# The root of three groups' norms as a power on GpSimd in a three-layer kernel

## The chip, the cores and the metric

The kernel runs on one core of a Trainium2 chip. The time is that of one execution on the device, in microseconds, and the number to predict is the median over several executions.

## The reference

Three layers follow one another. The first is attention over clusters: each query and each key is assigned to the centroid that its direction is nearest to, and a query sees only keys of its own cluster. The other two are networks over the 1536 tokens; the last mixes 8 experts with gates that are normalised in turns over rows and columns.

```python
B, H, S, D, C = 2, 8, 768, 64, 16
q_n = q / (np.linalg.norm(q, axis=-1, keepdims=True) + 1e-06)
k_n = k / (np.linalg.norm(k, axis=-1, keepdims=True) + 1e-06)
c_n = centroids / (np.linalg.norm(centroids, axis=-1, keepdims=True) + 1e-06)
q_assign = np.argmax(np.einsum('bhsd,hcd->bhsc', q_n, c_n), axis=-1)
k_assign = np.argmax(np.einsum('bhsd,hcd->bhsc', k_n, c_n), axis=-1)
mask = q_assign[:, :, :, None] == k_assign[:, :, None, :]
scores = np.where(mask, scale * np.matmul(q, k.transpose(0, 1, 3, 2)), -1e9)
attn = np.exp(scores - max); attn = attn / (sum(attn) + 1e-09); out = attn @ v
...
h = x @ w_in; r = np.maximum(h, 0.0); x = (s * (r * r) + b) @ w_out
...
for e in range(E): out += P[:, e:e+1] * (np.maximum(x @ w1[e], 0.0) @ w2[e])
```

## The kernel before

The work has two stages. The attention stage takes the first 280 us or so, the two networks the rest; the networks are almost only matrix products.

In the attention stage the 16 heads of the two batches make four groups of four heads (`n` = 0 to 3 in the code; the first to fourth group here). Every head has six query tiles of 128 rows, so there are 96 tiles, `g` = 0 to 95, and a group lasts 24 of them. `tile_steps(g)` issues for each tile: `row_max` two tiles ahead (VectorE, L454), `expo` one tile ahead (ScalarE, L461), `transp` (TensorE, L476), `score` three tiles ahead (TensorE, L448), the copy of the transposed weights out of PSUM in a rounded high part on ScalarE (`ath`, L483) and a remainder on VectorE (`atl`, L489), and a third of the product with the values (TensorE, L501). A score tile `s` has two buffers in PSUM, so the next score but one waits until `expo` has read its tile.

Before a group's heads can be scored their queries and keys have to be assigned. `prepare(n)` does it: it rounds the inputs into `hi` and `lo`, multiplies with the centroids (`sims`, L282), turns the result (`turn`, L290), scales it with the inverse norms (`normal`, L297), takes the maximum over the clusters (`top`, L301), marks where it is reached (`match`, `back`, `earliest`) and stacks `hi`, `lo` and the marks into `qa`, `qb`, `ka`, `kb` by transfers from SBUF to SBUF (`stack`, L331; those of the third and fourth head of the first group are issued from GpSimd's queue, all others from SP's).

`norms(n)` gives the inverse norms of a group in a tile `rn` of 128x48: it loads the group's queries and keys a second time with rows on partitions, squares them, sums over the 64 columns (`total`, L229 to L234, on GpSimd, VectorE or both, by group), takes the root (`root`, L237, on ScalarE), adds 1e-6 and inverts (`inverse`, L240 and L243, on VectorE). The first two groups' norms are made before the first tile; the second group's `inverse` is issued just ahead of tile 0's work, and its addition is held in program order:

```python
def root():
    nc.scalar.activation(rn, rn, AF.Sqrt)

def inverse():
    add = nc.vector.tensor_scalar_add(rn, rn, 1e-6)
    if n == 1:
        self.tc.keep_in_program_order(add)
    nc.vector.reciprocal(rn, rn)
```

For the third and fourth group these steps are put between the tiles by a table of offsets: `root` at tile 25 for the third group and at tile 50 for the fourth, `inverse` after it. ScalarE evaluates a function from a table that has to be loaded first (ACT_TABLE_LOAD): the root's and the exponent's are different tables; in this trace copies and squares cause no load. Each engine runs its instructions in a fixed order. Up to tile 71 a scheduler makes that order from the program and its dependencies; from there on the program's order is kept.

Of the kernel before, what the change touches and what calls it, by code (L numbers as in the profile page):

```python
# [8 lines left out]
F32 = mybir.dt.float32  # L9
# [3 lines left out]
AF = mybir.ActivationFunctionType  # L13
ALU = mybir.AluOpType
# [3 lines left out]
P = 128  # L18
# [44 lines left out]
class Kernel:  # L63
# [88 lines left out]
    def more_constants(self):  # L152
        nc, per = self.nc, self.per
        self.ones = per.tile([P, P], F32, name="ones")
        nc.gpsimd.memset(self.ones, 1.0)
        self.sb = per.tile([P, 2], F32, name="sb")
        self.wg = per.tile([P, KT, NE], F32, name="wg")
        self.wgs = per.tile([P, KT, 2, NE], F32R, name="wgs")
# [43 lines left out]
    def norms(self, n, soon=False):  # L202

        nc = self.nc
        rn = self.rn[n] = self.tile("rn", [P, 24, 2], bufs=2, pool=self.prep)
        nats = {}

        def load(u):
            if n == 1:
                nats[u] = self.tile("atl" if u else "ath", [P, 12, 2, D], bufs=2)  # L210
            else:
                nats[u] = self.tile("nat", [P, 12, 2, D], bufs=2, pool=self.prep)
            b, t = divmod(n, 2)
            nc.sync.dma_start(nats[u], self.qkn[b, t, :, 12 * u : 12 * u + 12])

        def square(u):
            nat = nats[u]
            if soon:
                nc.scalar.activation(nat, nat, AF.Square)
            else:  # L220
                nc.gpsimd.tensor_tensor(nat, nat, nat, op=ALU.mult)

        def total(u):
            nat = nats.pop(u)
            width = D
            while width > (1, 1, D, D // 2)[n] and n:
                width //= 2
                add = nat[:, :, :, :width]
                nc.gpsimd.tensor_tensor(add, add, nat[:, :, :, width : 2 * width], op=ALU.add)  # L229
            out = rn[:, 12 * u : 12 * u + 12]  # L230
            if width == 1:
                nc.gpsimd.tensor_copy(out.unsqueeze(3), nat[:, :, :, :1])
            else:
                nc.vector.reduce_sum(out, nat[:, :, :, :width], axis=AX.X)  # L234

        def root():
            nc.scalar.activation(rn, rn, AF.Sqrt)  # L237

        def inverse():
            add = nc.vector.tensor_scalar_add(rn, rn, 1e-6)  # L240
# [4 lines that stand above are left out]
        return load, square, total, root, inverse  # L245

    def prepare(self, n, soon=False):
# [886 lines left out]
```

## Time and profile before

| | |
|---|---|
| median of 3 runs | 1570.52 us (1570.37 to 1571.54) |
| the profiled execution | 1570.48 us |
| its span, first to last instruction | 1568.7 us |
| TensorE busy | 1526.6 us (97%) |
| VectorE busy | 898.7 us (57%) |
| ScalarE busy | 760.3 us (48%) |
| GpSimd busy | 964.6 us (61%) |
| ACT_TABLE_LOAD on ScalarE | 6, of 1283 ns each |
| mean granted clock of TensorE | 0.995 of full speed |

In the rows further down, PE is TensorE, DVE VectorE, ACT ScalarE and POOL GpSimd. A line of the timeline has the start in us, the duration in us, the engine, the line of the code, the operation, output and inputs by the program's names, the shapes, and how many instructions it merges; in brackets stands how long the engine sat idle before it and what ended that.

### The profile page before, as it was taken

Reading aid. Unit: us, or ns where it says so; the run is one execution under the profiler, and the core shown is the slowest. Engines: PE = TensorE matmul, PEld = TensorE weight load, DVE = VectorE, ACT = ScalarE, POOL = GpSimd, SP = SyncE. Lnnn points to the kernel's source line nnn. Section 1 sums busy time; section 2 is a strip of 40 time slices with the busy share of each in tenths; the row PEclk is TensorE's granted clock in tenths of the full one; section 3 lists DMA queues with packets and bytes.
Section 4 is the critical chain, followed back from the end, with each engine's and each line's share of the span. In section 5 each row is a group of like instructions: output and inputs, shape, how many; then the busy total and the mean of one; then the engine's idle time right before and its main releaser. Section 6 shows DMA issues by size and latency. Waiting matters only on the chain.

```text
span 1568.7 us, 21863 instructions
## 1 busy us (share of the span) xinstructions
PE 1526.6 (97%) x8136; PEld 1399.6 (89%) x8136; DVE 898.7 (57%) x1573; ACT 760.3 (48%) x1416; POOL 964.6 (61%) x726
## 2 busy tenths in 40 slices
PE   4999998999999999999999999999999999999998
PEld 4888987999999988899999999999999999999997
DVE  7989889876653445644444535565445444444444
ACT  4889898866665643343333333333333333333331
POOL 5764446656664866656566666677565757575652
PEclk8999999999999999999999999999999999999999
DMA  9864440122220011112121211213121212121211
GB/s 276 196 188 102 97 125 29 54 81 81 81 108 0 1 55 68 67 54 81 56 80 58 77 66 69 78 57 121 55 81 55 81 55 81 54 81 55 81 55 41
DMA packets 26793, 124.69 MB, mean 79 GB/s; under 512 B 4448, under 2 KB 4576, under 8 KB 16448
## 3 DMA queue, kind: packets, MB, share of 16 engines
q1 hardware_dynamic: 26112, 120.95, 23.9%
q0 software_dynamic: 576, 2.36, 0.7%
q8 instruction: 64, 1.05, 0.3%
q14 instruction: 41, 0.34, 0.1%
HBM read 99.80 MB, written 3.15 MB: 66 GB/s over the span
## 4 chain that ended last, share of the span: by engine, by line
PE 87%; ACT 4%; DVE 3%; POOL 2%; issue 2%; DMA 1%; SPq 0%; ACTq 0%; POOLq 0%; DVEq 0%
PE t L135 34%; PE s L985 22%; PE y L985 11%; PE s L705 7%; PE s L448 3%; PE pv L501 3%; PE u L135 2%; PE t L476 2%; ACT e L461 1%; PE u L476 1%; DVE atl L489 1%; DVE m L454 1%; ACT ath L483 1%; POOL fa L623 0%; DMA ka<-hi 0%
## 5 line engine op out<-in xcount | busy, mean ns | idle before, releaser
L964 ACT ACTIVATE hh<-c 128x384 fp32r<-128x384 f32 x256 | 134.6, 526 | 606.1 <-PE y L985 266.4
L892 POOL TENSOR_TENSOR wl<-raw,wh 128x1024 fp32r<-128x1024 f32 x64 | 155.3, 2427 | 348.2 <-ACT wh L891 348.2
L965 DVE SCALAR_TENSOR_TENSOR hl<-c,hh 128x384 fp32r<-128x384 f32 x256 | 174.8, 684 | 172.5 <-ACT hh L964 172.5
L985 PE MATMUL s<-wh,hh 128*128 128x512 f32 x512 | 201.2, 393 | 0.0
L985 PE MATMUL s<-wl,hh 128*128 128x512 f32 x512 | 200.6, 392 | 0.0
L985 PE MATMUL s<-wh,hl 128*128 128x512 f32 x512 | 200.3, 391 | 0.0
L135 PE MATMUL t<-th,ah 128*128 128x384 f32 x512 | 171.8, 336 | 0.8 <-DVE c L1059 0.8
L135 PE MATMUL t<-tl,ah 128*128 128x384 f32 x512 | 172.0, 336 | 0.0
L135 PE MATMUL t<-th,al 128*128 128x384 f32 x512 | 171.8, 336 | 0.0
L884 POOL TENSOR_TENSOR al<-sm,ah 128x1024 fp32r<-128x1024 f32 x64 | 156.6, 2447 | 3.5 <-ACT ah L881 3.4
L882 POOL TENSOR_TENSOR al<-raw,ah 128x768 fp32r<-128x768 f32 x64 | 137.8, 2153 | 0.0
L135 PE MATMUL t<-xh,ah 128*128 128x384 f32 x384 | 129.4, 337 | 0.1
L135 PE MATMUL t<-xh,al 128*128 128x384 f32 x384 | 129.2, 336 | 0.0
L135 PE MATMUL t<-xl,ah 128*128 128x384 f32 x384 | 129.0, 336 | 0.0
L1035 DVE TENSOR_TENSOR c<-t,c 128x384 f32<-128x384 f32 x64 | 35.7, 558 | 144.9 <-PE t L135 144.9
L985 PEld LDWEIGHTS s<-wh,hl 128*128 128x128 f32 x512 | 96.1, 188 | 21.1
L985 PEld LDWEIGHTS s<-wh,hh 128*128 128x128 f32 x512 | 96.2, 188 | 11.7
L985 PEld LDWEIGHTS s<-wl,hh 128*128 128x128 f32 x512 | 96.2, 188 | 11.3
L691 POOL TENSOR_TENSOR hl<-r,hh 128x384 fp32r<-128x384 f32 x64 | 74.3, 1162 | 49.3 <-ACT r L690 46.1
L985 PE MATMUL y<-wh,hl 128*128 128x512 f32 x256 | 99.7, 390 | 0.0
L985 PE MATMUL y<-wh,hh 128*128 128x512 f32 x256 | 99.7, 389 | 0.0
L985 PE MATMUL y<-wl,hh 128*128 128x512 f32 x256 | 99.6, 389 | 0.0
(231 smaller groups left out, 4019.2 us busy)
## 6 DMA issues: line engine op xcount, KB each, us to landing
raw<-in_w SPq DMA_DIRECT2D x64, 1024.0 KB, 4.8
wraw<-in_w SPq DMA_DIRECT2D x16, 1024.0 KB, 4.9
raw<-in_qk SPq DMA_DIRECT2D x15, 384.0 KB, 5.1
ka<-hi SPq DMA_DIRECT2D x28, 192.0 KB, 3.7
nat<-in_qkn SPq DMA_DIRECT2D x6, 768.0 KB, 7.7
vraw<-in_v SPq DMA_DIRECT2D x8, 384.0 KB, 4.8
out<-x SPq DMA_DIRECT2D x12, 256.0 KB, 2.0
qa<-hi SPq DMA_DIRECT2D x14, 192.0 KB, 2.6
```

Of the source, the lines that this page charges most:

```text
L135: self.nc.tensor.matmul(out, a, b, start=(i == 0), stop=(i == n - 1))
L448: nc.tensor.matmul(s[:, u, :HALF], a[:, qs], k[:, u * HALF : u * HALF + HALF], start=(a is qa), stop=(a is qb))
L476: nc.tensor.transpose(t[:, k, :], e[:, kt * P : kt * P + P], self.ident)
L501: nc.tensor.matmul(o, vt[:, kt].rearrange("p a d -> p (a d)"), aT[half][w][:, kt, :], start=(kt == 0 and w == 0), stop=(kt == QT - 1 and w ...
L691: nc.gpsimd.tensor_tensor(hl, r, f32(hh), op=ALU.subtract)
L705: nc.tensor.matmul(o, a, b, start=(start and i == 0), stop=(stop and i == 2))
L882: nc.gpsimd.tensor_tensor(al[:, : 3 * Q], raw[:, : 3 * Q], f32(ah[:, : 3 * Q]), op=ALU.subtract)
L884: nc.gpsimd.tensor_tensor(al[:, 3 * Q :], self.sums.rearrange("p a b -> p (a b)"), f32(ah[:, 3 * Q :]), op=ALU.subtract)
L892: nc.gpsimd.tensor_tensor(wl, raw[:, 1024:], f32(wh), op=ALU.subtract)
L964: nc.scalar.activation(hh, c, AF.Relu)
L965: nc.vector.scalar_tensor_tensor(hl, c, 0.0, f32(hh), op0=ALU.max, op1=ALU.subtract)
L985: nc.tensor.matmul(ys[t][m], a, b, start=(start and i == 0), stop=(stop and i == 2))
```

## The change

The root of the second to fourth group is a power of 0.5 on GpSimd, element by element, with a column of 0.5 spread over the tile. The first group's root and that of the centroids' norms stay on ScalarE.

```diff
@@ more_constants
         self.ones = per.tile([P, P], F32, name="ones")
         nc.gpsimd.memset(self.ones, 1.0)
+        self.half = per.tile([P, 1], F32, name="half")
+        nc.gpsimd.memset(self.half, 0.5)
@@ norms
         def root():
-            nc.scalar.activation(rn, rn, AF.Sqrt)
+            if n:
+                nc.gpsimd.tensor_tensor(rn, rn, self.half.unsqueeze(2).to_broadcast([P, 24, 2]), op=ALU.pow)
+            else:
+                nc.scalar.activation(rn, rn, AF.Sqrt)
```

The line numbers below the second hunk rise by five: L237 becomes L240 and L242, L240 becomes L245, L448 L453, L454 L459, L461 L466, L483 L488.

The order of GpSimd at the second group's root, just before tile 0, with what each instruction waits for (`atl` is the buffer of squares, `qa` and `ka` are stacked heads); before:

```order
L229 TENSOR_TENSOR atl<-atl 128x24 [waits Pool_49]
L232 COPY rn<-atl 128x24 [waits Pool_49]
L331 DMA qa<-hi_116 64x768
L331 DMA qa<-lo_118 64x768 [waits DVE_49]
L331 DMA ka<-hi_120 64x768 x2
```

and now:

```order
L231 TENSOR_TENSOR atl<-atl 128x24 [waits Pool_49]
L234 COPY rn<-atl 128x24 [waits Pool_49]
L240 TENSOR_TENSOR rn<-rn,half 128x48 [waits Pool_49]
L336 DMA qa<-hi_118 64x768
L336 DMA qa<-lo_120 64x768 [waits DVE_49]
L336 DMA ka<-hi_122 64x768 x2
```

The power stands between the last sum and the transfers. On VectorE the instructions of the same place, `inverse` of the second group and the first row maxima behind it, keep their order:

```order
L344 CAST kb<-eq 16x768
L245 TENSOR_SCALAR rn<-rn 128x48 [waits Pool_49]
L248 RECIPROCAL rn<-rn 128x48 [waits DVE_49]
L459 TENSOR_REDUCE m<-s 128x1 [waits PE_49] x3
L494 TENSOR_TENSOR atl<-u,ath 128x3x128 [waits Activation_49]
```

Only the addition's wait is another: it was for ScalarE and is for GpSimd.

The order of ScalarE at the third group's root, about tile 25; before:

```order
L237 ACT_TABLE_LOAD
L237 ACTIVATE rn<-rn 128x48
L483 CAST ath<-t 128x3x128 x2
L461 ACT_TABLE_LOAD
L461 ACTIVATE e,sums_65<-s,m 128x768
L483 CAST ath<-u 128x3x128
L461 ACTIVATE e,sums_65<-s,m 128x768
L526 COPY xb<-pv 64x384
L534 COPY rs<-t 64x384
L483 CAST ath<-t 128x3x128
L483 CAST ath<-u 128x3x128
L268 CAST hi_1265<-raw 128x768
```

with the third exponential right behind these rows, and now:

```order
L488 CAST ath<-t 128x3x128 x2
L531 COPY xb<-pv 64x384
L466 ACTIVATE e,sums_65<-s,m 128x768
L488 CAST ath<-u 128x3x128
L466 ACTIVATE e,sums_65<-s,m 128x768
L539 COPY rs<-t 64x384
L488 CAST ath<-t 128x3x128
L488 CAST ath<-u 128x3x128
L466 ACTIVATE e,sums_65<-s,m 128x768
L488 CAST ath<-t 128x3x128
L273 CAST hi_1267<-raw 128x768
```

Both loads and the root are gone, the copy into `xb` stands ahead of the first exponential, and the rounding into `hi` behind the third. The fourth group's root has lost its two loads in the same way.

The order of VectorE at the third group's `top` (`mx`), about tile 33; before:

```order
L454 TENSOR_REDUCE m<-s 128x1
L509 RECIPROCAL rsum<-rsum 128x3
L240 TENSOR_SCALAR rn<-rn 128x48
L243 RECIPROCAL rn<-rn 128x48
L528 TENSOR_TENSOR xb<-pv,xb 64x384
L290 STREAM_TRANSPOSE sim<-t 128x384
L489 TENSOR_TENSOR atl<-u,ath 128x3x128
L489 TENSOR_TENSOR atl<-t,ath 128x3x128
L454 TENSOR_REDUCE m<-s 128x1
L301 TENSOR_REDUCE mx<-sim 128x48
```

and now, behind the same row maximum:

```order
L533 TENSOR_TENSOR xb<-pv,xb 64x384
L514 RECIPROCAL rsum<-rsum 128x3
L236 TENSOR_REDUCE rn<-nat 128x24
L295 STREAM_TRANSPOSE sim<-t 128x384
L494 TENSOR_TENSOR atl<-u,ath 128x3x128
L494 TENSOR_TENSOR atl<-t,ath 128x3x128
L459 TENSOR_REDUCE m<-s 128x1
L494 TENSOR_TENSOR atl<-t,ath 128x3x128
L494 TENSOR_TENSOR atl<-u,ath 128x3x128
L459 TENSOR_REDUCE m<-s 128x1
L513 TENSOR_REDUCE rsum<-sums_64 128x3
L306 TENSOR_REDUCE mx<-sim 128x48
```

The maximum over the clusters comes one row maximum later, the fourth group's `inverse` has moved behind it, out of these rows, and a sum of that group's squares has come in from earlier. The order of the transfers on SP's queue is the same in both.

## Rows read from the trace of the kernel before

**Rows 1.** Busy time by stretches: length, PE, PEld, DVE, ACT, POOL, clock, DMA, GB/s.

```profile
345.00:1565.00 1220.00, 1216.39 (x6259) 1115.28 (x6257) 598.84 (x1039) 482.24 (x829) 766.53 (x551) 1.00 0.18 65
```

**Rows 2.** Timeline, all engines, 27 to 31.7 us: the second group's root and tile 0.

```profile
27.15 0.22 POOL L232 COPY rn<-atl 128x24 f32<-128x24 f32 x1
...
27.40 0.24 ACT L237 ACTIVATE rn<-rn 128x48 f32<-128x48 f32 x1 [6.08 <-POOL rn L232]
...
28.54 0.19 DVE L240 TENSOR_SCALAR rn<-rn 128x48 f32<-128x48 f32 x1
...
29.61 1.82 DVE L454 TENSOR_REDUCE m<-s 128x1 f32<-128x768 f32 x2 [0.39 <-PE s L448]
...
30.61 0.90 ACT L461 ACTIVATE e<-s,m 128x768 f32<-128x768 f32 x1 [1.67 <-DVE m L454]
...
31.65 0.69 PE L448 MATMUL s<-ka,qa 128*128 128x384 f32 x1 [1.44 <-ACT e L461]
```

**Rows 3.** Timeline of ScalarE, 92.3 to 97.6 us: the third group's root.

```profile
92.31 1.28 ACT L237 ACT_TABLE_LOAD   x1
93.61 0.24 ACT L237 ACTIVATE rn<-rn 128x48 f32<-128x48 f32 x1
94.19 0.99 ACT L483 CAST ath<-t 128x384 fp32r<-128x384 f32 x2 [0.34 <-PE t L476]
95.20 1.28 ACT L461 ACT_TABLE_LOAD   x1
96.49 0.90 ACT L461 ACTIVATE e<-s,m 128x768 f32<-128x768 f32 x1
```

**Rows 4.** Timeline of TensorE: two waits for an exponential.

```profile
41.06 0.44 PE L448 MATMUL s<-ka,qa 128*128 128x384 f32 x1 [1.46 <-ACT e L461]
...
97.54 0.86 PE L448 MATMUL s<-ka,qa 128*128 128x384 f32 x2 [1.70 <-ACT e L461]
```

**Rows 5.** Busy time by stretches, columns as in rows 1.

```profile
41.00:42.00 1.00, 0.94 (x7) 0.92 (x8) 1.00 (x3) 1.00 (x3) 0.19 (x1) 1.00 0.95 234
...
95.84:97.54 1.70, 0.00 (x1) 0.00 (x1) 1.70 (x5) 1.69 (x4) 0.00 (x0) 1.00 0.91 168
97.54:101.10 3.56, 3.56 (x14) 3.37 (x14) 2.57 (x6) 2.62 (x6) 0.44 (x1) 0.53 0.39 162
101.10:103.47 2.37, 1.89 (x13) 1.58 (x12) 1.42 (x2) 2.16 (x5) 1.37 (x2) 0.99 0.01 3
```

**Rows 6.** Timeline, VectorE, ScalarE and TensorE, 96 to 104 us.

```profile
96.67 0.95 DVE L234 TENSOR_REDUCE rn<-nat 128x24 f32<-128x768 f32 x1
...
98.77 0.48 ACT L526 COPY xb<-pv 64x384 f32<-64x384 f32 x1
...
101.69 0.84 ACT L268 CAST hi<-raw 128x768 fp32r<-128x768 f32 x1
...
103.47 0.61 PE L448 MATMUL s<-ka,qa 128*128 128x384 f32 x2 [0.48 <-ACT e L461]
```

**Rows 7.** Behind the fourth group's root: TensorE's wait (timeline), and the stretch before it.

```profile
126.51 0.62 PE L448 MATMUL s<-ka,qa 128*128 128x384 f32 x2 [0.40 <-ACT e L461]
...
113.00:125.00 12.00, 12.00 (x78) 10.95 (x76) 11.18 (x23) 10.44 (x20) 8.82 (x8) 1.00 0.40 139
```

**Rows 8.** GpSimd's instructions by line and shape: count, busy us, mean ns of one.

```profile
L221 POOL TENSOR_TENSOR nat<-nat 128x1536 f32<-128x1536 f32 x4 | 11.1, 2772 | 1.8 <-DMA nat<-in_qkn 1.8
...
L229 POOL TENSOR_TENSOR atl<-atl 128x48 f32<-128x48 f32 x1 | 0.3, 267 | 0.1
```

**Rows 9.** Timeline of GpSimd and VectorE behind the third and fourth group's roots.

```profile
94.44 1.00 POOL L352 TENSOR_TENSOR vv<-vraw,vv 128x384 fp32r<-128x384 f32 x1 [2.38 <-PE t L476]
...
119.79 0.83 POOL L297 TENSOR_TENSOR sim<-sim,rn 128x384 f32<-128x384 f32 x1
...
120.84 0.92 DVE L301 TENSOR_REDUCE mx<-sim 128x48 f32<-128x768 f32 x1
...
123.63 0.95 DVE L454 TENSOR_REDUCE m<-s 128x1 f32<-128x768 f32 x1
```

## Prediction

> **What bounds the kernel now.** I read three views. The table by stretches first: from 345 to 1565 us TensorE (PE) is busy 1216 of 1220 us [rows 1], so the two expert layers gain nothing by themselves; whatever the attention stage gains or loses before them reaches the end one for one, since all later work follows from it. Then the timeline around the three roots that move. And last the clock of TensorE in those places.
>
> At the **start** (second group) ScalarE has been waiting 6.08 us for GpSimd's sum of squares; its root then takes 0.24 us [rows 2]. VectorE, in its fixed order, adds 1e-6 at 28.54, when it has just finished copying the marker rows, and inverts; the first row maximum follows at 29.61, after 0.39 us of waiting for TensorE's score. The first exponential at 30.61 waits for that maximum and for nothing else, so the exponent's table load in between is hidden, and TensorE's third score at 31.65 waits for the exponential. This is the path.
>
> At the **third group's root** ScalarE loads the root's table (1.28), takes the root, waits 0.34 for transposes, copies two, and loads the exponent's table (1.28) before the exponential at 96.49 [rows 3]. TensorE waits 1.70 for that exponential before the score at 97.54 [rows 4], and then its granted clock falls: mean 0.53 of full speed from 97.54 to 101.10, that is mostly the lower of its two levels, 1.2 against 2.4 GHz [rows 5]. An earlier wait of the same kind, 1.46 us at 41.06, was followed by a microsecond at clock 1.00 [rows 4, 5].
>
> At the **fourth group's root** TensorE is busy in all 12 us from 113 to 125 [rows 7], so the two loads there only make ScalarE late; it shows as a wait of 0.40 at 126.51.
>
> **The change, part by part.** The sum is made against the profiled execution, 1570.48 us (span 1568.7 and 1.78 around it); the median of the runs is 1570.52, the same for this purpose.
>
> *The table loads.* ScalarE loses three roots of 0.24 us and four loads of 1.28 us, 5.9 us in all. The roots of the first group and of the centroids stay, and with them the load of the root's table and one of the exponent's, which can now run before 27 us, hidden as it is today. What lies on the path:
> - Third group, first load: the copies after it wait for transposes anyway [rows 3], so it gives nothing. Cover gone, it would be 0.9 more.
> - Second load: the exponential could start at 95.20 instead of 96.49. The new order puts a 0.48 us copy of the output ahead of it, which stood behind it [rows 6]. So it starts 1.29 - 0.48, about 0.83 earlier with the gaps, and TensorE waits 0.87, not 1.70.
> - Clock: a wait of 0.87 is shorter than the 1.46 that left the clock at 1.00. 3.56 us at 0.53 is 1.89 us of work at full clock, so 1.67 comes back.
> - The exponential after that stands behind an 0.84 us rounding of the next heads, and TensorE waits 0.48 for it at 103.47 [rows 6]; the new order puts that rounding behind it: 0.48.
> - Sum 0.83 + 1.67 + 0.48 = 2.98. What is late next is VectorE: in the 7.63 us of those three stretches it is busy 5.69 [rows 5], and 0.95 of that, a sum of squares of the fourth group [rows 6], now comes later. 4.74 has to fit into 7.63 - 2.98 = 4.65, so it just does.
> - Fourth group: 0.40 [rows 7].
>
> The gain is 3.4 us. With nothing of it but the 0.83 it is 0.8; with all 5.9 on the path it is 5.9.
>
> On the price of a load, the row has the root starting 0.02 us after the load's end and the load right behind a copy [rows 3]. The Trainium skill (ScalarE: Activation LUTs, What ACT_TABLE_LOAD costs) has about 1283 ns and a drain of about 1380 ns for each switch. The load agrees with the row; the drain doesn't appear here. By the page's figure the one exposed load would give an estimated 1.4 us more.
>
> *The power on GpSimd.* Three tensor-tensor powers on 128x48, of a duration d that no row shows. Below, a power can't be cheaper than an addition of that shape, 0.27 us [rows 8]. The dearest simple row is a product of 128x1536 at 2.77 us: 32 passes over 48 columns. A power in software is a logarithm and an exponential, each a chain of products and sums with a split into exponent and mantissa; I take some 30 such passes, d = 2.5 us. Two such chains of 30 passes, 5.5 us, is my upper end. This is the weakest number here.
>
> What waits for it:
> - Second group. The power follows the copy that ends at 27.37, so it ends at 27.44 + d. VectorE's addition is next in its order and would start at 28.54; behind it are the reciprocal and the row maxima. The maximum has 0.39 us to spare [rows 2]. So the path is late by S = 27.44 + d + 0.05 - 28.54 - 0.39 = d - 1.44. For d = 2.5 that is 1.06; for 0.27, nothing; for 5.5, 4.06. Nothing gives it back: the score, exponential and transposes follow one another from there.
> - Queued behind it on GpSimd are the twelve transfers that stack heads 2 and 3. They are late by d, but those heads are first scored at step 9, some 20 us later (25 steps take from 30.61 to the third group's root at 93.61, 2.5 us each). Nothing.
> - Third group: GpSimd waits 2.38 before its next instruction at 94.44 [rows 9], and in the new order VectorE adds 1e-6 about four row maxima later. Nothing up to some 7 us.
> - Fourth group: the power stands ahead of the product that now starts at 119.79. VectorE's maximum over it, now at 120.84, comes in the new order after the row maximum of 123.63 [rows 9]. So about 123.63 + 0.95 - 119.79 - 0.83, 4 us, are free; beyond that, d - 4.
> - The column of 0.5 is one memset early on GpSimd, while that engine waits for its first operands. Nothing.
>
> *Sum:* 1570.48 - 3.4 + 1.06 = **1568.1 us**.
>
> **The rivals.**
> 1. *A cheap power* (d up to 1.44). Nothing waits, and the gain is whole: 1570.48 - 3.4 = 1567.1. For it: additions of 128x48 take 0.27. Against it: a power is no addition. With all of ScalarE's 5.9 on the path, 1564.6. Chance 0.26.
> 2. *The gain is hidden.* VectorE has only 0.1 us to spare by the sum above, and the order of TensorE and VectorE is also shuffled from 90 to 150 us. If the clock falls again or VectorE is late, 0.83 is left: 1570.48 - 0.8 + 1.06 = 1570.7. Against it: each wait named is for ScalarE. Chance 0.14.
> 3. *A long power; slower.* VectorE stands still at 28.54 with everything behind it, and again at the fourth group. The loss is d - 1.44 and, beyond 4 us, d - 4 more. It passes the 3.4 at d = 4.4 and is 3.1 us beyond it at d = 6. At 5.5 the time is 1570.48 - 3.4 + 4.06 + 1.5 = 1572.6; at 10, 1570.48 - 3.4 + 8.56 + 6 = 1581.6. For it: the operation is software, 48 columns long, and on the path. Against it: it needs more than twice my price. Chance 0.18. A rule speaks for it by itself: the Trainium skill (GPSIMD Engine Reference, Instruction dispatch) says that the first call of freshly loaded GpSimd code pays some 6 us with no instruction to show for it. No run here shows that yet. If it held for this first power, the estimate by the page is 4.1 us slower than before.
>
> That the loads stay is excluded: the new order of ScalarE has none at these roots.
>
> **How the numbers follow.** My forecast has 0.42. About 0.2%, 3.1 us, is what a measurement of this kernel can tell from no change, so faster means under 1567.4 and slower over 1573.6. The forecast lies 0.7 us inside "same"; an error of one microsecond in gain or d carries it over: 0.16 faster, 0.26 same. The cheap power gives 0.16 faster, 0.10 same. The hidden gain gives 0.13 same, 0.01 slower. The long power gives 0.01 same, 0.17 slower. Sums: faster 0.32, same 0.50, slower 0.18. The range runs from 1565.0, the cheap power with nearly all of ScalarE's time, to 1573.5, d = 5.5 with a gain a little short; outside is most of the long power and little else.
>
> **What would show it.** The power's row on GpSimd gives d at once; VectorE's addition at the start should begin at its end, and the first exponential at 30.61 + d - 1.44. There should be two table loads, both before 30 us. Before the score that now stands at 97.54 TensorE should wait under 1 us, with the clock at 1.00 for the next 4 us. By 130 us the work should be 2.3 us ahead, and stay so. I am wrong if d is over 4.4, if the clock falls again near 97, or if a wait for VectorE takes the place of the one for ScalarE.

## The result and the profile after

The changed kernel takes 1584.43 us (median of 4 runs, 1584.03 to 1585.72), the kernel before on the same chip 1570.44: a ratio of 1.0083, with a 95% interval of 1.0069 to 1.0097 (the quotient of the two medians is 1.0089). It is 14.0 us slower where 2.4 us faster was forecast, and lies outside the range. The profiled execution took 1584.03 us with a span of 1582.1.

Busy time by engine on the page of the changed kernel:

```profile
PE 1527.5 (97%) x8136; PEld 1400.1 (88%) x8136; DVE 945.8 (60%) x1573; ACT 754.6 (48%) x1409; POOL 986.6 (62%) x730
```

ScalarE has lost 5.7 us, GpSimd gained 22.0, less than the 24.5 of its three powers, and VectorE 47.1, though the change gives it no work; that is taken up at the end of this section.

The price of the power comes next. The groups of GpSimd's instructions by line (count, busy us, mean ns of one):

```profile
L240 POOL TENSOR_TENSOR rn<-rn,half 128x48 f32<-128x48 f32 x3 | 24.5, 8158 | 0.1
```

One power of 128x48 takes 8.16 us, not 2.5; the addition of the same shape takes 0.27 and the dearest simple product 2.77 [rows 8].

The timeline of the changed kernel at the second group's root, all engines (start, duration, engine, line, operation, shapes; in brackets the idle time before it and what ended that):

```profile
27.07 0.22 POOL L234 COPY rn<-atl 128x24 f32<-128x24 f32 x1
...
27.37 8.40 POOL L240 TENSOR_TENSOR rn<-rn,half 128x48 f32<-128x48 f32 x1
...
35.81 0.19 DVE L245 TENSOR_SCALAR rn<-rn 128x48 f32<-128x48 f32 x1 [7.37 <-POOL rn L240]
...
36.40 1.75 DVE L459 TENSOR_REDUCE m<-s 128x1 f32<-128x768 f32 x2
...
37.33 0.90 ACT L466 ACTIVATE e<-s,m 128x768 f32<-128x768 f32 x1 [15.73 <-DVE m L459]
```

Before, the addition started at 28.54 and the first exponential at 30.61 [rows 2]. Now VectorE stands 7.37 us at the addition with the row maxima behind it, and the exponential is 6.72 us late.

The third group's root has no load any more. ScalarE's timeline there, and TensorE's one wait between 98 and 112 us:

```profile
102.29 0.48 ACT L531 COPY xb<-pv 64x384 f32<-64x384 f32 x1
102.79 0.90 ACT L466 ACTIVATE e<-s,m 128x768 f32<-128x768 f32 x1
```

```profile
103.84 0.61 PE L453 MATMUL s<-ka,qa 128*128 128x384 f32 x2 [1.13 <-ACT e L466]
```

TensorE waits 1.13 us where it waited 1.70 [rows 4]. The stretches below (length, then busy us of PE, PEld, DVE, ACT and POOL, the clock, DMA share, GB/s) show the clock at 1.00 behind that wait, where it was 0.53 [rows 5], and a clock of 0.54 in a place further on, which the kernel before doesn't have:

```profile
100.00:110.00 10.00, 8.87 (x60) 8.02 (x59) 9.25 (x18) 8.63 (x18) 9.81 (x4) 1.00 0.66 159
...
136.39:140.00 3.61, 3.61 (x15) 3.44 (x16) 3.46 (x7) 1.97 (x5) 3.01 (x4) 0.54 0.02 5
...
345.00:1565.00 1220.00, 1216.92 (x6268) 1117.40 (x6267) 646.08 (x1041) 489.58 (x839) 773.16 (x556) 1.00 0.18 65
```

In the expert layers TensorE is as busy as before [rows 1]. Ahead of the second stretch it stands still for 6.43 us. The timelines of GpSimd, VectorE and TensorE there:

```profile
122.97 1.00 POOL L540 TENSOR_TENSOR x<-xb,rs 64x384 f32<-64x384 f32 x1 [2.12 <-DVE rsum L514]
123.94 2.13 POOL L269 TENSOR_SCALAR raw<-raw 128x768 f32<-128x768 f32 x1
126.05 8.03 POOL L240 TENSOR_TENSOR rn<-rn,half 128x48 f32<-128x48 f32 x1
134.05 0.83 POOL L302 TENSOR_TENSOR sim<-sim,rn 128x384 f32<-128x384 f32 x1
```

```profile
128.19 0.15 DVE L513 TENSOR_REDUCE rsum<-sums 128x3 f32<-128x6 f32 x1
134.91 0.95 DVE L306 TENSOR_REDUCE mx<-sim 128x48 f32<-128x768 f32 x1 [6.58 <-POOL sim L302]
```

```profile
136.39 0.90 PE L481 MATMUL t<-cst,e 128*128 128x128 f32 x3 [6.43 <-DVE atl L494]
```

The fourth group's power is ahead of the third group's product `sim` on GpSimd. VectorE waits 6.58 us for that product, the remainder `atl` stands behind VectorE's maximum, and TensorE waits 6.43 for `atl`. Behind that wait its clock is 0.54, mostly the lower of its two levels, until 140 us.

A ledger follows from the start times of the 96 exponentials, changed against before. The difference is +7.08 us up to tile 23, +4.59 at tile 30 (third group's loads gone), +3.21 at tile 34 (fourth group's loads), +12.02 at tile 37 (the wait for `sim` and the low clock), +11.48 at tile 95, the end of the attention stage. And then it grows, in layers whose code is the same. These are the first and last of ScalarE's 64 copies of `c` in the expert layer, before and after:

```profile
557.76 0.47 ACT L1024 COPY c<-t 128x384 f32<-128x384 f32 x1
...
1542.10 0.47 ACT L1024 COPY c<-t 128x384 f32<-128x384 f32 x1
```

```profile
568.95 0.47 ACT L1029 COPY c<-t 128x384 f32<-128x384 f32 x1
...
1555.64 0.47 ACT L1029 COPY c<-t 128x384 f32<-128x384 f32 x1
```

From +11.19 to +13.54: 2.35 us that no step had. The group of instructions that stands out there is the remainder `hl` on VectorE, 684 ns before and 871 after; its busy time rises by 47.9 us, about as much as that of VectorE as a whole:

```profile
L965 DVE SCALAR_TENSOR_TENSOR hl<-c,hh 128x384 fp32r<-128x384 f32 x256 | 174.8, 684 | 172.5 <-ACT hh L964 172.5
```

```profile
L970 DVE SCALAR_TENSOR_TENSOR hl<-c,hh 128x384 fp32r<-128x384 f32 x256 | 222.7, 871 | 164.6 <-ACT hh L969 164.6
```

### The profile page after: what moved, and what is told of

The parts are those of the page before. It is cut to its first block, busy times and chain, and to the rows that moved or that the text cites. A ratio compares the mean times of both kernels' runs of the same rounds, so it can differ in the third digit from the quotient of the medians.

```text
span 1582.1 us, 21860 instructions
## 1 busy us (share of the span) xinstructions
PE 1527.5 (97%) x8136; PEld 1400.1 (88%) x8136; DVE 945.8 (60%) x1573; ACT 754.6 (48%) x1409; POOL 986.6 (62%) x730
## 4 chain that ended last, share of the span: by engine, by line
PE 86%; DVE 4%; ACT 4%; POOL 3%; issue 2%; DMA 1%; SPq 0%; ACTq 0%; POOLq 0%; DVEq 0%
PE t L135 34%; PE s L990 22%; PE y L990 11%; PE s L710 7%; PE s L453 3%; PE pv L506 3%; PE u L135 2%; PE t L481 2%; ACT e L466 1%; DVE atl L494 1%; POOL rn L240 1%; DVE m L459 1%; PE u L481 1%; ACT ath L488 1%; DMA ath<-in_qkn 1%
## 5 line engine op out<-in xcount | busy, mean ns | idle before, releaser
L970 DVE SCALAR_TENSOR_TENSOR hl<-c,hh 128x384 fp32r<-128x384 f32 x256 | 222.7, 871 | 164.6 <-ACT hh L969 164.6
L889 POOL TENSOR_TENSOR al<-sm,ah 128x1024 fp32r<-128x1024 f32 x64 | 166.1, 2595 | 3.9 <-ACT ah L886 3.8
L887 POOL TENSOR_TENSOR al<-raw,ah 128x768 fp32r<-128x768 f32 x64 | 127.0, 1984 | 0.0
```

The costliest lines, as they stand in the source:

```text
L887: nc.gpsimd.tensor_tensor(al[:, : 3 * Q], raw[:, : 3 * Q], f32(ah[:, : 3 * Q]), op=ALU.subtract)
L889: nc.gpsimd.tensor_tensor(al[:, 3 * Q :], self.sums.rearrange("p a b -> p (a b)"), f32(ah[:, 3 * Q :]), op=ALU.subtract)
L970: nc.vector.scalar_tensor_tensor(hl, c, 0.0, f32(hh), op0=ALU.max, op1=ALU.subtract)
```

## Experiments

Differences at a tile are start times of its exponential against the kernel before, profile against profile; "attention's end" is tile 95. Ratios are to the kernel before on the same chip, with 95% intervals; they differ a little from the quotient of the medians. One profile stands against one profile here: a run further down with no power and the old order (the one with an unused tile of 64 bytes) differs by 2.1 us at attention's end, so a difference of that size at one tile shows little by itself.

### One power at a time, and none

```diff
-            if n:
+            if n == 1:
```

and `n == 2` and `n == 3` in the two runs after it.

Second group alone:

> The power for the second group alone; the third and fourth group's roots are on ScalarE as before. Theory A (waits: VectorE stands in program order behind an 8-us power): the first exponentials come 6.7 to 7.1 us later, nothing is taken back after it, +7.0 us, 1577.4. Theory B (not the wait, but something spread over the program, such as GpSimd and VectorE slowing each other, or the slow growth seen in the expert stages): a third of the 14.0 us lost, +4.7, 1575.1, and a difference that still grows by about 2 us after 560 us.

Measured 1579.29 us, ratio 1.0053 (1.0041 to 1.0065). VectorE's timeline:

```profile
35.38 0.19 DVE L245 TENSOR_SCALAR rn<-rn 128x48 f32<-128x48 f32 x1 [7.38 <-POOL rn L240]
```

The difference is +6.29 at tile 0 and +6.18 at attention's end: the wait, and nothing given back. Theory A holds there (it had 6.7 to 7.1), but the time has 2 us more than it says.

Third group alone:

> The power for the third group alone. Theory A: two table loads fall away at 92 to 96 us, the power hides, -2.5 us as read from the exponentials of tiles 24 to 30 of the changed kernel, 1567.9; no growth in the expert stages. Theory B: +4.7 less the 2.5 us of the loads, +2.2, 1572.6.

Measured 1574.28, ratio 1.0024 (1.0012 to 1.0036). The loads' gain is there, -2.48 at tile 30, and is lost by tile 35 (+0.16); the end is at +0.84. The fourth group's loads, which this run keeps, come between two exponentials that are now earlier; ScalarE's timeline:

```profile
120.84 1.28 ACT L466 ACT_TABLE_LOAD   x1
122.13 0.90 ACT L466 ACTIVATE e<-s,m 128x768 f32<-128x768 f32 x1
```

This exponential (tile 33) was at 122.36 before: whatever was gained ahead of it is gone. The further 0.8 to the end come between tiles 42 and 48 and weren't taken apart. Again 2 us more come after the attention.

Fourth group alone:

> The power for the fourth group alone. Theory A: 1.4 us gained where the loads were, then VectorE waits for the product sim behind the power; by the changed kernel's exponentials at tile 35 the loss there is 8.4, so +7.0, 1577.4; by the prediction's formula, power less 4 us of slack, +2.6, 1573.0. Theory B: +4.7 less 1.4, +3.3, 1573.7, without a wait of VectorE for sim of over 4 us.

Measured 1578.86, ratio 1.0049 (1.0035 to 1.0062); +5.98 at attention's end, from +1.06 at tile 30. GpSimd's and VectorE's timelines:

```profile
115.34 8.05 POOL L240 TENSOR_TENSOR rn<-rn,half 128x48 f32<-128x48 f32 x1 [0.56 <-DVE rn L236]
123.38 0.83 POOL L302 TENSOR_TENSOR sim<-sim,rn 128x384 f32<-128x384 f32 x1
```

```profile
123.43 0.83 DVE L245 TENSOR_SCALAR rn<-rn 128x48 f32<-128x48 f32 x1 [5.37 <-POOL rn L240]
...
128.12 0.95 DVE L306 TENSOR_REDUCE mx<-sim 128x48 f32<-128x768 f32 x1 [1.11 <-POOL sim L302]
```

Here VectorE waits for the power itself, 5.37 us at the inverse, and 1.11 for `sim`. With the other powers in place the same time is lost behind `sim` alone. It is one cause with two places.

A product in the place of the power:

```diff
-                nc.gpsimd.tensor_tensor(rn, rn, ..., op=ALU.pow)
+                nc.gpsimd.tensor_tensor(rn, rn, ..., op=ALU.mult)
```

> A product with 0.5 stands in the place of the power for all three groups, so the root is left out there; order, places and loads are those of the changed kernel. Theory A: all waits go, the loads stay away: about 0.8 at the start, 2.5 and 1.4 at the loads, -4.7 us, 1565.7; no growth in the expert stages. Theory B (the growth of 2 us after 560 us comes with the change and not with the power's length): 1567.7, with that growth. If the gain at the loads is given back later: 1570.4.

Measured 1571.14, ratio 1.0005 (0.9996 to 1.0014). The attention ends at -1.64, and yet the time isn't shorter: 2 us are lost after it, as in all four runs, with `hl` at 864 ns. So that loss is not the power's. It comes with something that all four share, and they share the new constant tile.

### The constant alone, and the waits moved

The kernel before with the tile added and unused:

```diff
+        self.half = per.tile([P, 1], F32, name="half")
+        nc.gpsimd.memset(self.half, 0.5)
```

> The kernel before with nothing but the new constant: a tile of 128x1 (4 bytes in each partition), filled with 0.5 and used by nobody. All four runs with parts of the change had the remainder hl of the expert stages at 864 ns on VectorE against 684 before, and lost about 2 us after 300 us. Theory C (the 4 bytes move all later tiles to other addresses in SBUF): hl at about 864 ns, attention unchanged, +2.2 us, 1572.7. Theory D (the growth comes from the power, from the instruction order or from the run): hl at 684 ns, 1570.5.

Measured 1573.12, ratio 1.0013 (1.0004 to 1.0022). The attention ends at +0.01; then:

```profile
557.26 0.47 ACT L1026 COPY c<-t 128x384 f32<-128x384 f32 x1
...
1543.92 0.47 ACT L1026 COPY c<-t 128x384 f32<-128x384 f32 x1
```

```profile
L967 DVE SCALAR_TENSOR_TENSOR hl<-c,hh 128x384 fp32r<-128x384 f32 x256 | 230.1, 900 | 165.3 <-ACT hh L966 165.2
```

From -0.50 to +1.82, 2.32 us, with no power and, but for the tile's own fill, the same order on every engine: theory C.

The changed kernel with `[P, 2]` in the place of `[P, 1]`:

> The changed kernel with the constant as a tile of 128x2 (8 bytes), of which the first column is used; nothing else differs. Theory C: hl back at 684 ns and 2.2 us less, 1582.2. Theory D: 1584.4. If 8 bytes move the tiles just as badly: 1584.4 with hl at 864 ns.

Measured 1585.10, ratio 1.0089 (1.0076 to 1.0103), `hl` at 889 ns: 8 bytes move the tiles as 4 do. In the compiled programs tiles start at multiples of 32 bytes.

The waits moved, all powers kept (8-byte constant):

```diff
+                if n == 3:
+                    self.tc.keep_in_program_order(p)
...
-        norm1[4]()
+        plan.setdefault(3, []).append([norm1[4]])
```

> All three powers stay, at 8 us each, with the constant of 8 bytes; the second group's inverse is issued after tile 3 instead of ahead of tile 0, and the fourth group's power is held in program order, so that it stands behind both products sim of the third group. Theory A (the loss is the two waits behind the power): both go; what is left is the gain of the product version, -1.6 at the end of the attention, 1568.9; no VectorE wait for the power or for sim of over 1 us. Rival (8 us on GpSimd cost the same wherever they stand, by what queues behind them or by GpSimd and VectorE slowing each other): each power still costs 4 us or more, 1582 or more. Halfway (the third group's sim is 8 us later and takes back its loads' gain, as in the run with the third group alone): 1571.3.

Measured 1575.35, ratio 1.0024 (1.0010 to 1.0038); both waits of VectorE are gone, 10 us less than the changed kernel with the same constant. But the difference jumps from +0.09 at tile 5 to +4.86 at tile 6. GpSimd's and ScalarE's timelines:

```profile
35.79 0.76 POOL L338 DMA_DIRECT2D qa<-hi  x1
...
41.29 0.52 POOL L338 DMA_DIRECT2D qb<-hi  x1
```

```profile
49.08 0.83 ACT L275 CAST hi<-raw 128x768 fp32r<-128x768 f32 x1 [5.25 <-DVE m L461]
```

The maximum named had ended long before; the rounding of the second group's inputs into `hi` has to wait until the transfers have read the first group's `hi` (one buffer). The last of them is issued at 41.29 and takes 7.6 us to land by the table of DMA issues.

The second group on ScalarE, the fourth's power held back:

```diff
-            if n:
+            if n > 1:
```

> As the run with the waits moved, but the second group's root is on ScalarE and its inverse where it was. Theory A: the same time but for what the start gains, 0.3 us or so: 1569.2. Rival of costs wherever the power stands: two powers, 1578 or more. If it is below the other by over 1 us, the power beside the first tiles costs there.

Measured 1571.17, ratio 1.0011 (0.9998 to 1.0024); +0.10 at tile 6, -2.23 at tile 30, -1.14 at the end, then 2 us lost to the tile.

### 64 bytes, and the transfers first

```diff
+        self.half = per.tile([P, 16], F32, name="half")
```

in the kernel before, unused:

> The kernel before with an unused constant tile as in the run with the tile alone, but 64 bytes in each partition instead of 4. The compiled programs place tiles at multiples of 32 bytes: with 4 or 8 bytes all later tiles of the left side move by 32 (hh from 74912 to 74944, hl from 81056 to 81088) while c stays at 174048; with 64 they move by 64. Theory C in this form (what counts is how hh and hl lie to c within 64 bytes): hl back at about 684 ns and 1570.5. Rival (any move of the tiles from where they were tuned, or the tile's own fill, costs): hl at 864 to 901 ns, 1572.5.

Measured 1577.61, ratio 1.0041 (1.0027 to 1.0055). I was wrong on the form of the theory: it is worse, not better. First and last copy of `c`:

```profile
555.10 0.47 ACT L1026 COPY c<-t 128x384 f32<-128x384 f32 x1
...
1546.46 0.47 ACT L1026 COPY c<-t 128x384 f32<-128x384 f32 x1
```

```profile
L967 DVE SCALAR_TENSOR_TENSOR hl<-c,hh 128x384 fp32r<-128x384 f32 x256 | 251.8, 984 | 169.7 <-ACT hh L966 169.6
```

From -2.66 to +4.36: 7.02 us. VectorE still idles 170 us for `hh`, so `hl` isn't short of time. TensorE runs the same 4932 products between the two copies and idles 3.1 us in both kernels; it is the products that take longer, 988.21 us against 981.25. By stretches (columns as in rows 1), before and then in this run:

```profile
557.76:1542.10 984.34, 981.25 (x4932) 886.25 (x4931) 473.85 (x851) 347.64 (x599) 624.44 (x450) 1.00 0.19 68
```

```profile
555.10:1546.46 991.36, 988.21 (x4932) 887.72 (x4931) 549.65 (x851) 347.57 (x599) 619.78 (x450) 1.00 0.19 68
```

What makes `hl` longer is in the traces too. Some 50 of its 256 instructions start within 0.07 us of GpSimd's remainder `al<-raw,ah`. One such pair before, then one in this run:

```profile
1003.27 0.55 DVE L965 SCALAR_TENSOR_TENSOR hl<-c,hh 128x384 fp32r<-128x384 f32 x1
1003.33 2.19 POOL L882 TENSOR_TENSOR al<-raw,ah 128x768 fp32r<-128x768 f32 x1
```

```profile
1003.88 1.85 POOL L884 TENSOR_TENSOR al<-raw,ah 128x768 fp32r<-128x768 f32 x1
1003.91 2.24 DVE L967 SCALAR_TENSOR_TENSOR hl<-c,hh 128x384 fp32r<-128x384 f32 x1
```

Before, `hl` starts first in all 49 pairs and takes under 0.6 us; here `al` starts first in 48 of 50, and `hl` takes over 2 us, to 0.4 us past the end of `al`. With the tile of 4 bytes it is 29 of 49. Elsewhere `hl` is no longer than before. So `hl` shows which of the two started first, a matter of tens of nanoseconds; it doesn't show why TensorE's products are longer, and no run tells that.

The attention of this run ends 2.10 us early, though its engines run the old order with both table loads. Most of that comes at tile 26. TensorE waits for the exponential behind the third group's second load as long as it did before, and yet the clock behind the wait is 1.00, not 0.53 [rows 4, 5]:

```profile
97.08 0.61 PE L450 MATMUL s<-ka,qa 128*128 128x384 f32 x2 [1.71 <-ACT e L463]
...
97.08:100.64 3.56, 3.56 (x23) 3.25 (x24) 3.07 (x8) 3.51 (x8) 0.98 (x1) 1.00 0.40 162
```

The changed kernel with the same constant:

> The changed kernel with its constant as a tile of 64 bytes in each partition, nothing else differs. Theory C: hl at about 684 ns, the attention as in the changed kernel (+11.5 at its end), no growth after it, 1582.2. Rival: 1584.4 and hl at 864 ns or more.

Measured 1589.45, ratio 1.0114 (1.0097 to 1.0131): the growth in the expert layer is 7.04 (+12.06 to +19.10). It adds to the attention's loss and doesn't mix with it.

The second group's power behind the transfers, in the run with the waits moved and with the 64-byte constant; this power is held in program order too (that line is left out here):

```diff
-        norm1[3]()
...
-        norm1[4]()
+        plan.setdefault(0, []).append([norm1[3]])
+        plan.setdefault(7, []).append([norm1[4]])
```

> As the run with the waits moved, with the 64-byte constant, and the second group's power stands behind the eleven or so transfers of the third and fourth head on GpSimd's queue instead of ahead of them; its inverse is issued after tile 7. Theory A2 (with VectorE's wait gone, the power still held back those transfers by 8.5 us, so that the tiles hi they read came free late and ScalarE's rounding of the second group's inputs waited 5.2 us: +4.8 at tile 6): the step at tile 6 falls from +4.8 to 0.5 or less, attention's end at -0.5 to -1.6, 1569 to 1570. Rival (the 4.8 us are the power itself, by slowing VectorE or the transfers under way): still 4 us or more by tile 10, 1573 or more.

Measured 1581.84, ratio 1.0067 (1.0051 to 1.0083), some 7 us of it the tile. The jump at tile 6 is gone (+0.17), so it was the transfers. But tile 10 is at +5.68; GpSimd's and TensorE's timelines:

```profile
39.39 8.36 POOL L240 TENSOR_TENSOR rn<-rn,half 128x48 f32<-128x48 f32 x1
47.73 1.81 POOL L280 TENSOR_TENSOR lo<-raw,hi 128x768 fp32r<-128x768 f32 x1
```

```profile
58.08 0.69 PE L289 MATMUL u<-lo,z 128*128 128x384 f32 x1 [2.10 <-POOL lo L280]
```

Now the remainders `lo` stand behind the power, and TensorE, whose order has their product with the centroids ahead of the transposes, waits. So the transfers were the step at tile 6, as theory A2 has it, and the rival is right too that the start loses over 4 us by tile 10.

The third and fourth group's powers, 64-byte constant:

> The power for the third and fourth group alone, the fourth's held in program order, as in the run with the second group on ScalarE, with the 64-byte constant. Theory C: that run's -1.1 at the end of the attention stays to the end, 1569.3, and this is the fastest version so far, by 0.1% or less. Rival (the growth is given back in another way): 1571.

Measured 1577.06, ratio 1.0038 (1.0023 to 1.0053); attention's end at +0.10, and 7.02 lost after it. The order of instructions is that of the run with the second group on ScalarE, and yet tile 6 differs by 1.9 us.

### No tile moved, and the power in pieces

The 0.5 goes into a spare column of `cst`:

```diff
-        cst = per.tile([P, 2 * P + 1], F32, name="cst")
+        cst = per.tile([P, 2 * P + 2], F32, name="cst")
+        self.half = cst[:, 2 * P + 1 :]
```

(The fill with 0.5 and the load of the old columns alone are left out here.)

The changed kernel with that:

> The changed kernel with the 0.5 in a spare column of the tile cst, which has 28 unused bytes behind it, so that no other tile moves (hh at 74912, hl at 81056 as before). Theory C2 (the new tile moved hh and hl, and the further from their old place the slower the expert stages: 684 ns and +0 at 0 bytes, 880 and +2 at 32, 987 and +7 at 64): hl at 684 ns, the attention at +11.5 as in the changed kernel, nothing added after it, 1582.0. Rival (the expert stages are slowed by something else that the change brings): 1584.4.

Measured 1582.37, ratio 1.0071 (1.0058 to 1.0084), with

```profile
L970 DVE SCALAR_TENSOR_TENSOR hl<-c,hh 128x384 fp32r<-128x384 f32 x256 | 174.2, 682 | 172.4 <-ACT hh L969 172.4
```

and +12.49 at the first copy of `c`, +12.50 at the last. The growth is the place of the tiles, and nothing else in the change. (The attention's end, +12.5, is 1.0 above the changed kernel's in this profile; the low clock behind the wait for `sim` lasts past 140 us here.)

Two powers, no tile moved:

> The power for the third and fourth group, the fourth's held in program order, the second group's root on ScalarE, and the 0.5 in cst, so that no tile moves. Theory C2: -1.1 at the end of the attention as in the run with the 4-byte... 8-byte constant, and it stays: 1569.4, hl at 684 ns. Rival: 1571.

Measured 1568.81, ratio 0.9991 (0.9982 to 0.9999): faster than before by 1.6 us, with an interval that only just leaves out 1. (The profiled execution, 1571.07, is the second longest of the 12; it lost 2.2 us at tile 6, and its attention ends at +0.65, so no profile shows the gain.)

The fourth group's power in four:

```diff
+            part = rn if k is None else rn[:, 6 * k : 6 * k + 6]
...
+                    [(1 + k, root, k) for k in range(4)] + [(6, inverse)]
```

> As the last, with the fourth group's power cut into four of 128x12, held in program order at tiles 50 to 53, so that GpSimd's other work gets between. If the power's time goes by columns: 2.0 us a piece, the 1.4 us lost at tile 43 behind the whole power mostly gone, attention's end at -1.9 to -2.5, 1568.3. If a call costs the same whatever its columns: 8 us a piece and 1580 or more.

Measured 1578.25, ratio 1.0046 (1.0032 to 1.0059). GpSimd's groups of that line:

```profile
L244 POOL TENSOR_TENSOR rn<-rn,cst 128x12 f32<-128x12 f32 x4 | 9.0, 2267 | 0.0
L244 POOL TENSOR_TENSOR rn<-rn,cst 128x48 f32<-128x48 f32 x1 | 8.0, 8048 | 0.0
```

So 12 columns take 2.27 and 48 take 8.05: by a line through these two points, an estimate, 160 ns for a column and some 0.34 us beside. The 1.4 us behind the whole power at tile 43 are gone (-0.27 against +1.19). And at tile 54 there is a new loss of 7; VectorE's timeline:

```profile
175.26 0.97 DVE L249 TENSOR_SCALAR rn<-rn 128x48 f32<-128x48 f32 x1 [6.57 <-POOL rn L244]
```

That was my placing: the scheduler put the inverse where VectorE came to it before the last piece.

Both in pieces, the second group's between the remainders:

> All three powers on GpSimd as in the change, the second and fourth group's in four pieces of 128x12, the second group's issued behind the transfers (with the remainders lo in between) and its inverse after tile 7; no tile moves. Theory A3 (what a power costs is what queues behind it on GpSimd while that queue has no slack): the pieces delay each remainder by 2 to 6 us instead of 8; tile 10 at +0 to +2 instead of +5.7, attention's end at -2 to +0.5, 1568.5 to 1571. Rival (8 us of power at the start cost the same in pieces): +5.7 at tile 10, 1574.

Measured 1585.52, ratio 1.0095 (1.0081 to 1.0110). Tile 10 is at +6.88. From tile 8 it lost 5.5, as much as in one piece; 1.1 had come at tile 6. By tile 23 it is at +8.97, where one piece gave +6.33: three of the pieces lie between the remainders, and the last of these ends at 59.2, against 58.0 in one piece. The fourth group's inverse waits 6.57 here too. Attention's end is at +14.46. At the start the power costs as much in pieces: as far as these two runs show, the chain through the four remainders has no gap that holds one.

The product, no tile moved:

> The product in the place of all three powers (the root is left out), with the 0.5 in cst, so that no tile moves. It shows what the change could be worth if GpSimd had a root as cheap as a product: the loads' gain of the earlier product run, -1.6 at the end of the attention, with no loss after it: 1568.8. If the 1.5 us that run lost at tile 6 (a transfer that landed late) were chance, up to -3.1: 1567.3. If the tiles' place was not what took its gain: 1571.

Measured 1567.95, ratio 0.9989 (0.9977 to 1.0000); -1.68 at tile 30, -2.60 at the end, -2.66 at the last copy of `c`.

The pieces with a later inverse, held in program order:

```diff
-            if n == 1:
+            if n in (1, 3):
                 self.tc.keep_in_program_order(add)
...
-                    [(1 + k, root, k) for k in range(4)] + [(6, inverse)]
+                    [(1 + k, root, k) for k in range(4)] + [(9, inverse)]
```

> As the run with the fourth group's power in four pieces, but its inverse is held in program order at tile 57, behind the pieces. Theory A (in that run VectorE stood 6.6 us before the inverse for the last piece, and everything behind it): the 8.2 us lost from tile 54 on vanish, attention's end at 0 to -2, 1568.5, level with the two powers without a moved tile (1568.8) or up to 1.5 below. Rival (the pieces themselves hold GpSimd's sums and products, and these cost): still 4 us or more after tile 54, 1573 or more.

Measured 1568.74, ratio 0.9987 (0.9977 to 0.9997). VectorE's timeline:

```profile
181.09 0.16 DVE L249 TENSOR_SCALAR rn<-rn 128x48 f32<-128x48 f32 x1
```

The inverse doesn't wait, and tile 54 is at -0.73: the 8 us were that wait, and not the pieces. Among the kernels that take every root this is level with the two whole powers, and both are faster than the kernel before by some 0.1%, at the edge of what these runs can tell.

## Why the prediction was wrong

**The price.** "I take some 30 such passes, d = 2.5 us", with 5.5 as the upper end, failed by a factor of three: 8.0 to 8.4. It was called the weakest number, and it was; the 30 passes and the bound of two chains were a guess about software that no row supported, and no run shows what the 8 us consist of. The long power was the rival with 0.18, its worked case of 10 us giving 1581.6. At 8.0 the same formulas give 1570.5 - 3.4 + 6.6 + 4 = 1577.7. That leaves 6.3 us to the profiled 1584.0, which a right price would not have covered: 3.8 at the fourth group, 2.35 after the attention, and 0.2 from smaller errors that nearly cancel.

**The start.** "The path is late by d - 1.44" was right within 0.7 us: 8.40 - 1.44 = 6.96, measured 6.72 here and 6.29 with this power alone. **The transfers** at "nothing" were wrong, though: not because their heads are needed early, but because they free `hi`. The forecast looked at who reads what they write, and not at who overwrites what they read. In the changed kernel VectorE's wait covers it; when that was taken away 4.8 us appeared. The pieces show the same of the remainders.

On the first call the Trainium skill (GPSIMD Engine Reference, Instruction dispatch) has some 6 us for freshly loaded code, with no instruction to show for them. In this trace the first power starts 0.08 us after the copy's end and is 0.37 us longer than the third (8.40 against 8.03); no 6 us are seen, and no row shows whether its code was loaded just then. Nor is the 0.37 the price of a first power: where the first one comes at 115 us it takes 8.05, and a product in the second group's place is 0.36 longer than its successors as well (0.63 against 0.27). The prediction's estimate from that page is also mis-added: with 2.5 + 6 its formulas give 8.5 - 1.44 - 3.4 = 3.7 us slower, not 4.1.

**The third group.** The forecast was 2.98, measured 2.49 (tile 23 to 30). The exponential comes 0.78 earlier, where 0.83 was forecast. The clock stays at 1.00, which was the largest term; TensorE's wait is 1.13, not the 0.87 forecast. But the 1.67 for the clock rest on one profile. Of five that keep these loads, four have a clock of 0.52 to 0.56 behind a wait of 1.70 us, and the one with the unused 64 bytes has 1.00. In the fifteen without the loads the wait is at most 1.14 and the clock 1.00. So the term held, but the length of the wait alone doesn't decide it, as the forecast had it. That VectorE wouldn't wait for the power here held even at 8.05 us: the third group's addition at 113.13 follows without a gap.

**The fourth group.** The loads' 0.40 is small and doesn't last: in the product run without a moved tile the difference goes from -1.68 at tile 30 to about -2.0 at tiles 35 to 42, and is back at -1.69 at tile 53. "4 us are free" failed. The forecast let the power start where the product started, at 119.79. It started at 126.05, which against tile 30 (+4.59) is 1.7 us later: in GpSimd's new order the output `x` stands ahead of the scaling of `raw`, where it stood behind before, so the engine waits 2.12 us with the scaling and the power behind it. And VectorE had come to its maximum at 128.34. So only 8.03 + 0.83 - 6.58 = 2.3 us of the power and the product were covered, where the forecast covered 4 and the product, 4.8. And 6.4 us of idling on TensorE are followed by 3.61 us at a clock of 0.54, which no term had; by an estimate from that row full speed would have taken 1.95. In all the difference grows by 7.4 from tile 30 to 37, where 3.6 come from the forecast's formulas; the cover that was missing, 2.5, and the clock, 1.7, are about the rest.

**The sum.** The gain was right in kind, and a third of it wasn't there. The product run that keeps all tiles in place, which pays for no power, is 2.25 us faster than before; the forecast of 3.4 with nothing to pay for lacks 1.2. Its profile puts the gain together otherwise: 2.5 at the third group, and 0.8 between tiles 54 and 55 that no term had and no run took apart (VectorE's order differs there too). And 1.4 are lost at tile 6 (-0.58 to +0.86), a wait of ScalarE before it rounds a second group's input. That wait differs between runs by 0 to 2.6 us, also between runs with the same order. It goes with the landing of the transfers that free `hi`: those into `qb` from GpSimd's queue take 8.1 us (median, 30 to 50 us) before and in the run with the second group on ScalarE, where nothing is lost, 8.5 in this run, and 9.9 with two powers and no moved tile, which loses 2.2. Why they land later wasn't tried.

**The missing term.** "The two expert layers gain nothing by themselves" is true, and they lost 2.35. The edit "one memset early on GpSimd... Nothing" looked at the instruction and not at the tile. By the compiled programs, a 4-byte tile takes 32 bytes of the pool; `hh` moves from 74912 to 74944 and `hl` from 81056 to 81088, while `c` stays on the other side. Growth between the first and last copy of `c`: at most 0.05 us in the six profiles with no move, 2.3 to 2.5 in the nine with 32 bytes, 7.0 in the four with 64. That the place decides is shown; why TensorE's products take longer by it is not.

So of the 13.5 us between the two profiles, 7.1 are the wait at the start, -2.5 the third group's loads, +7.4 the fourth group with its loads and its wait, -0.8 the rest up to the first copy of `c` (nearly all of it between tiles 54 and 55), and 2.35 the moved tiles.

## What to carry to other kernels

An operation moved to an idle engine is paid by what queues behind it there, and by an engine in fixed order that waits for it with other work behind: shares of busy time say nothing on that, so ask for each queued instruction who reads its output and who overwrites its input. If a duration is in no row, treat it as unknown by a factor, and let the forecast follow from what happens at three times the guess. A term read off one profile, as the clock's 1.67 was, should be seen in a second one before it is counted. And a new tile, however small, moves the tiles after it: add constants into spare bytes, or compare against the old kernel with the empty tile alone.

## What was not expected of the hardware

A power on GpSimd takes 8.05 us for 128x48 and 2.27 for 128x12, some 160 ns for a column; 8.05 is 30 times an addition. By where tiles lie in SBUF, at 32 or 64 bytes' difference, the same 4932 products of TensorE took 2.3 or 7.0 us more in 984. VectorE's remainder `hl` took 0.55 us where it started just ahead of GpSimd's `al` (the kernel before), and over 2 where it started just behind it (64 bytes). And the same wait of 1.7 us on TensorE was followed by a clock of 0.53 in one run and of 1.00 in another with the same order.
